# Turning half of the attention's probability units with VectorE blocks and a DRAM round trip

## The chip, the cores and the metric

The kernel runs on one core of one Trainium2 chip. The metric is the device time of one execution in microseconds (us). Three runs of the kernel before gave 720.13, 720.44 and 720.46 us, a median of 720.44 us. The engines are named as the profile names them: PE is TensorE (PEld its weight loads), DVE is VectorE, ACT is ScalarE, POOL is GpSimd, and SP issues the DMAs; SPq is the DMA queue of SP.

## What is computed

Attention over a few global keys and a local window, then a mixture of four experts, then a gated layer with a norm. The change touches the attention alone, but the experts' matmuls are woven into the same stretch.

```python
def _attn_ref(q, k, v, n_global, n_local):          # B=2, H=8, S=768, D=64; 8 global keys, window of 96
    scores = scale * np.matmul(q, k.transpose(0, 1, 3, 2))
    keep = is_global | is_local
    scores = np.where(keep, scores + bias, -1e9)
    a = np.exp(scores - np.max(scores, axis=-1, keepdims=True))
    a = a / (np.sum(a, axis=-1, keepdims=True) + 1e-09)
    return np.matmul(a, v)

def _moe_ref(x, domain_probs, w1, w2):              # N=1536, D=512, E=4, F=1024
    for e in range(E):
        out += p[:, e:e + 1] * (np.maximum(x @ w1[e], 0.0) @ w2[e])
```

## The kernel before, in words

The 1536 tokens are 12 slots of 128. A unit is one slot and one pair of heads, so there are 48 units, four for each slot: unit u belongs to slot u // 4 (from unit 8 on). For a unit, PE multiplies queries by 256 keys into the PSUM tile `sps` (`scores`, L1219); DVE adds the bias and takes the row extreme (L1270, one instruction for each head); ACT takes the exponential and the row sum (L1277); DVE sums and inverts (L1256, L1257) and scales the probabilities `p` (L1261, 128x512); PE turns the four 128x128 chunks through PSUM (`stage_b`, L1301) and ACT copies them to SBUF (L1303); PE multiplies them by the values into `x` (`stage_c`, L1323; each fp32 product is two instructions); after the fourth unit of a slot ACT and DVE split `x` into a high and a low part, `xh` (L1334) and `xl` (L1335).

From unit 14 (`PAIRS`) on the loop takes two units in one step: step t (t = 14, 16, ..., 50) issues the scores and the softmax of units t and t+1, scales and turns units t-2 and t-1, and multiplies units t-4 and t-3 by their values. Between these, `pull(share)` draws matmuls of the experts from a generator, worth `share` ns at full speed, and does so twice in a step. The order of each engine's instructions is the order of the program; nothing is reordered. So a step divisible by 4 (16, 20, ...) begins a slot, and a step that leaves 2 (18, 22, ...) ends one: there `stage_c` completes the slot before.

SP carries the loads in program order. At the start of a step divisible by 4, `next_operands` loads keys (`load_keys`, L90, two DMAs, by the table LOAD_AFTER) and the queries (L1188) of a later slot. The keys lie in a ring of four places; keys 6 to 9 also need their first 32 columns, which POOL copies from the place of key 6 (L93). Key 6 is loaded in step 20. At the end of a step that leaves 2, `load_v` (L1193) loads a later slot's values into one of two buffers. From step 36 on POOL forms sums for the experts (`x_forms`, L799), a few at the end of each step.

Near the end of the kernel, `blocks` (L1036 to L1043) turns a 128x1024 tile in the same way as the change does: one DVE transpose in 32x32 blocks (L1038), one DMA to `t_dram` (L1040), four DMAs back (L1042).

Of the kernel before, what the change touches and what calls it, by code (L numbers as in the profile page):

```python
# [8 lines left out]
F32 = mybir.dt.float32  # L9
# [36 lines left out]
SHARE = {11: 1000}  # L46
HALF = 512
PAIRS = 14


@with_exitstack
def kernel(ctx, tc, ep, qk, vp, nn, pr, wall, w64, gl, out):
# [1094 lines left out]
    def fast_arm():  # L1147
        st = stream("f")
        with ExitStack() as es:
# [4 lines left out]
            b0 = tmp2.rearrange("p a (h c) -> p (a h) c", c=128)  # L1154
            qp = enter(tc.tile_pool(name="qp", bufs=3))
            vpl = enter(tc.tile_pool(name="vpl", bufs=2))
            pp = enter(tc.tile_pool(name="pp", bufs=4))
            ptp = enter(tc.tile_pool(name="ptp", bufs=4))
            ss = enter(tc.tile_pool(name="ss", bufs=4))
            hA = enter(tc.tile_pool(name="hA", bufs=4))  # L1160
            psg = enter(tc.tile_pool(name="psg", bufs=3, space=PSUM))
# [63 lines left out]
            def soft(u, first):  # L1225

                s, pr_ = unit(u)
                nch, boff, _ = geom(s)
                nw = 128 * nch
                p = pp.tile([128, 2, 256], F32, tag="p", name="p")  # L1230
                mn = ss.tile([128, 2], F32, tag="mn", name="mn")
                st_p[u], st_rs[u] = p, sum_of(u)
                norm = stage_n(u - 1) if st_rs.get(u - 1) is not None else iter(())
                if not first:
                    next(norm, None)
                for a in range(2):
                    h = 2 * pr_ + a
                    bias = b0[:, h] if boff is None else btab[:, h, boff:boff + 256]
                    nc.vector.tensor_tensor_reduce(out=p[:, a, :nw], in0=sps[:, a, u % 2, :nw], in1=bias, scale=-0.125,
                                                   scalar=3.0e38, op0=ALU.add, op1=ALU.min,  # L1240
                                                   accum_out=mn[:, a:a + 1])
                    if not first:
                        while a and late:
                            late.pop()()
                        next(norm, None)
                for a in range(2):
                    nc.scalar.activation(p[:, a, :nw], p[:, a, :nw], AF.Exp, bias=mn[:, a:a + 1], scale=-1.0,
                                         accum_out=st_rs[u][:, a, 0:1])
                return norm

            def soft_pair(t):

                if PAIRS < t <= NU:
                    st_rs.pop(t - 2), st_rs.pop(t - 1)
                    su = ss.tile([128, 4], F32, tag="su2", name="su2")
                    nc.vector.tensor_reduce(out=su, in_=sums[:, (t // 2 - 1) % 3], op=ALU.add, axis=AX.X)  # L1256
                    nc.vector.reciprocal(out=su, in_=su)  # L1257
                    for u in (t - 2, t - 1):
                        p = st_p[u]
                        st_last[0] = p[:, 0, 0:1]  # L1260
                        nc.vector.tensor_tensor(out=p, in0=p, in1=su[:, 2 * (u % 2):2 * (u % 2) + 2].unsqueeze(2)  # L1261
                                                .to_broadcast([128, 2, 256]), op=ALU.mult)
                for u in (t, t + 1) if t < NU else ():
                    s, pr_ = unit(u)
                    boff = geom(s)[1]
                    st_p[u] = p = pp.tile([128, 2, 256], F32, tag="p", name="p")
                    st_rs[u] = sum_of(u)
                    mn = ss.tile([128, 2], F32, tag="mn", name="mn")
                    for a in range(2):
                        nc.vector.tensor_tensor_reduce(out=p[:, a], in0=sps[:, a, u % 2],  # L1270
                                                       in1=btab[:, 2 * pr_ + a, boff:boff + 256], scale=-0.125,
                                                       scalar=3.0e38, op0=ALU.add, op1=ALU.min,
                                                       accum_out=mn[:, a:a + 1])
                    while late:
                        late.pop()()
                    for a in range(2):
                        nc.scalar.activation(p[:, a], p[:, a], AF.Exp, bias=mn[:, a:a + 1], scale=-1.0,  # L1277
                                             accum_out=st_rs[u][:, a, 0:1])
# [15 lines left out]
            def stage_b(u):  # L1294
                s, pr_ = unit(u)
                nch = geom(s)[0]
                p = st_p.pop(u)
                pt = psT.tile([128, 4, 128], F32, tag="pt", name="pt")
                for a in range(2):
                    for c in range(nch):  # L1300
                        nc.tensor.transpose(pt[:, nch * a + c], p[:, a, 128 * c:128 * c + 128], ident)  # L1301
                t = ptp.tile([128, 4, 128], F32, tag="pts", name="pts")
                nc.scalar.copy(t[:, :2 * nch], pt[:, :2 * nch])  # L1303
                st_pt[u] = t

            def stage_c(u):
                s, pr_ = unit(u)
                nch, _, parts = geom(s)
                t = st_pt.pop(u)
                if u < N0:  # L1310
                    x, place = x0[:, 2 * (pr_ % 2):2 * (pr_ % 2) + 2], s
                else:
                    if pr_ == 0:
                        st_x[s] = psX.tile([128, 4, 128], F32, tag="x", name="x")
                    x, place = st_x[s], pr_
                for c in range(nch):
                    for a in range(2):
                        h = 2 * pr_ + a
                        if s < NAT:
                            v = v0[:, s, 64 * h:64 * h + 64]  # L1320
                        else:
                            v = vts[s][:, parts[c], 64 * h:64 * h + 64]
                        nc.tensor.matmul(x[64 * a:64 * a + 64, place], lhsT=v, rhs=t[:, nch * a + c],  # L1323
                                         start=(c == 0), stop=(c == nch - 1))
                if u < N0 and s == NAT - 1:
                    xc = slice(pr_, pr_ + 1), slice(0, 128 * NAT)
                elif u >= N0 and pr_ == 3:
                    xc = slice(0, 4), slice(128 * s, 128 * s + 128)
                else:
                    return  # L1330
                h_, l_ = xh[:, xc[0], xc[1]], xl[:, xc[0], xc[1]]
                if u < N0:
                    x = x.rearrange("p s c -> p (s c)").unsqueeze(1)
                nc.scalar.copy(h_, x)  # L1334
                late.append(lambda: nc.vector.tensor_tensor(out=l_, in0=x, in1=h_.bitcast(F32), op=ALU.subtract))  # L1335
# [198 lines left out]
                    st.split_piece("act" if t < N0 + 12 and t % 2 else "dve", "pool")  # L1534
                    st.load_piece()
            for t in range(PAIRS, NU + 3, 2):
                share = 2 * (EARLY if t < N0 + 27 else 750)
                if t < NU:
                    for u in (t, t + 1):
                        scores(u)  # L1540
                    for u in (t, t + 1):
                        next_operands(*divmod(u, 4))
                soft_pair(t)
                while late:
                    late.pop()()
                while st.rests:
                    st.rests.pop(0)()
                if t <= NU:
                    st.behind = False
                    pull(share)  # L1550
                for _ in range(2):
                    next(rest_p, None)
                if t <= NU:
                    for u in (t - 2, t - 1):
                        stage_b(u)
                if t < NU:
                    tokens[0] = 128 * done
                    st.behind = t < NU - 2
                    if t > PAIRS:
                        pull(share)  # L1560
                for u in (t - 4, t - 3):
                    if u in st_pt:
                        stage_c(u)
                if t % 4 == 2:
                    done = (t - 2) // 4
                    load_v(done + 1)
                if t == 4 * 8 + 4:
                    st.forms = st.x_forms(lambda: [tmp2[:, k] for k in range(2)])
                if st.forms and t < NU:
                    nc.gpsimd.tensor_copy(out=flg[:, 0:1], in_=st_last[0])  # L1570
                    for f in st.forms.pop(0):
                        f()
                if t < NU:
                    for u in (t, t + 1):
                        st.split_piece("act" if u < N0 + 12 and u % 2 else "dve", "pool")
                        st.load_piece()
# [180 lines left out]
```

## Time and profile before

| what | value |
|---|---|
| median of the runs | 720.44 us |
| profiled execution, its time | 720.14 us |
| profiled execution, its span from first to last instruction | 718.3 us |
| granted TensorE clock over the span | 1.000 |
| busy share of PE, DVE, ACT, POOL | 99%, 71%, 43%, 45% |
| steps 16 to 50 of the attention | from about 37 to 127 us of the span |

The span is 1.9 us shorter than the execution's time; that remainder lies around the instructions. The chain that ended last is followed back from the last instruction. The timeline gives start and duration of each instruction, merged where the same ones follow each other; a busy PE is modelled, so the start of the next instruction tells more than the end of one. In a row, the bracket names how long the engine was idle before the instruction, and what ended that.

### The profile page before, as it was taken

The page shows a single profiled execution, that of the slowest core. Times are in us where ns is not written, and L with a number is a line of the kernel's source. Part 1 is how long each engine was busy: PE and PEld are TensorE (multiplying, and loading weights), DVE is VectorE, ACT ScalarE, POOL GpSimd, SP SyncE. Part 2 cuts the span into 40 slices and gives each one's busy share as a digit, 9 for nine tenths or more (in the row PEclk, how much of TensorE's full clock was granted, in tenths as well). Part 3 has the DMA queues.
Part 4 walks back from the last instruction along what each step waited for, and adds up shares of the span by engine and source line. Part 5 has one row for each costly group of instructions (what it writes and reads, how often), then busy time and mean ns, then how long its engine had stood idle before and what let it go on. Part 6 is the DMA issues. An engine that isn't in the chain of part 4 may idle for free.

```text
span 718.3 us, 11137 instructions
## 1 busy us (share of the span) xinstructions
PE 709.4 (99%) x3863; PEld 591.7 (82%) x3863; DVE 506.5 (71%) x1100; ACT 307.0 (43%) x688; POOL 323.2 (45%) x389
## 2 busy tenths in 40 slices
PE   7999999999999999999999999999999999999997
PEld 5788877888888889888888988888898888888886
DVE  6788857638785685676668578857965667778870
ACT  5877765422523333232343324325334324454452
POOL 6700143574793165228307423630735089555600
PEclk9999999999999999999999999999999999999999
DMA  8734311320352324234133323323232780334341
GB/s 250 169 119 133 119 45 45 103 73 18 116 170 65 108 76 125 73 102 114 51 118 104 101 74 117 118 74 104 93 98 74 267 347 1 122 114 132 108 128 49
DMA packets 55601, 79.32 MB, mean 110 GB/s; under 512 B 5744, under 2 KB 33648, under 8 KB 55536
## 3 DMA queue, kind: packets, MB, share of 16 engines
q1 hardware_dynamic: 54976, 78.10, 34.4%
q8 instruction: 32, 0.52, 0.3%
q10 hardware_dynamic: 560, 0.43, 0.2%
q14 instruction: 33, 0.27, 0.1%
HBM read 59.60 MB, written 18.90 MB: 109 GB/s over the span
## 4 chain that ended last, share of the span: by engine, by line
PE 97%; DVE 1%; ACT 1%; issue 0%; DVEq 0%
PE fg L582 37%; PE fg L759 19%; PE fo L1087 9%; PE fh L988 8%; PE fg L674 7%; PE fg L551 6%; PE x L1323 3%; PE sps L1219 3%; PE pt L1301 3%; PE g L1343 1%; PE wp L133 1%; DVE fg L687 1%; ACT fhh L643 1%; PE fh L1068 0%; PE sps L1212 0%
## 5 line engine op out<-in xcount | busy, mean ns | idle before, releaser
L582 PE MATMUL fg<-fhh,wV 128*128 128x512 f32 (+1 forms) x800 | 243.4, 384 | 0.4
L582 PEld LDWEIGHTS fg<-fhh,wV 128*128 128x128 f32 x800 | 148.3, 188 | 33.5 <-issue 3.3
L582 PE MATMUL fg<-fhl,wV 128*128 128x512 f32 (+1 forms) x400 | 149.1, 381 | 0.0
L582 PEld LDWEIGHTS fg<-fhl,wV 128*128 128x128 f32 x400 | 74.9, 188 | 15.2 <-DVE su L1257 0.3
L643 ACT ACTIVATE fhh<-fg 128x512 fp32r<-128x512 f32 x80 | 47.5, 598 | 66.6 <-DVE fg L769 40.3
L308 POOL TENSOR_TENSOR wR<-kr,wR 128x512 fp32r<-128x512 f32 (+1 forms) x28 | 29.0, 1060 | 97.0 <-ACT wR L300 97.0
L644 DVE SCALAR_TENSOR_TENSOR fhl<-fg,fhh 128x512 fp32r<-128x512 f32 x80 | 54.0, 686 | 6.9 <-ACT fhh L643 5.4
L601 POOL TENSOR_TENSOR scr<-scr,kr 128x512 f32<-128x512 f32 x24 | 31.0, 1291 | 61.4 <-DVE kr L600 61.4
L759 PE MATMUL fg<-xt,fwS 128*128 128x512 f32 x252 | 58.3, 389 | 0.0
L759 PEld LDWEIGHTS fg<-xt,fwS 128*128 128x128 f32 x252 | 47.3, 188 | 9.8
L759 PE MATMUL fg<-xh,wR 128*128 128x512 f32 x168 | 54.0, 389 | 0.0
L769 DVE TENSOR_TENSOR fg<-kr,fg 128x512 f32<-128x512 f32 x42 | 29.0, 693 | 33.0 <-PE fg L759 22.6
L596 DVE TENSOR_TENSOR fg<-fg,pb 128x512 f32<-128x512 f32 x59 | 40.9, 692 | 14.4 <-PE fg L582 13.4
L1277 ACT ACTIVATE p<-p,mn 128x256 f32<-128x256 f32 x68 | 33.9, 499 | 22.9 <-DVE mn L1270 22.8
L597 DVE TENSOR_TENSOR scr<-fg,scr 128x512 f32<-128x512 f32 x59 | 40.8, 692 | 2.0
L551 PE MATMUL fg<-xh,wR 128*128 128x512 f32 (+1 forms) x128 | 39.4, 373 | 0.0
L759 PEld LDWEIGHTS fg<-xh,wR 128*128 128x128 f32 x168 | 31.6, 188 | 6.5
L308 POOL TENSOR_TENSOR fwS<-kr,fwS 128x512 fp32r<-128x512 f32 x28 | 35.7, 1299 | 1.6 <-ACT fwS L300 1.6
L1087 PE MATMUL fo<-xt,fhh 128*128 128x512 f32 (+1 forms) x156 | 35.4, 375 | 0.0
L764 ACT COPY kr<-fg 128x512 f32<-128x512 f32 x42 | 24.2, 590 | 25.6 <-PE fg L759 25.6
L759 PE MATMUL fg<-xl,wR 128*128 128x512 f32 x84 | 32.7, 389 | 0.0
L1087 PEld LDWEIGHTS fo<-xt,fhh 128*128 128x128 f32 x156 | 27.6, 188 | 5.1
(283 smaller groups left out, 1492.3 us busy)
## 6 DMA issues: line engine op xcount, KB each, us to landing
w_dram<-fr SPq DMA_DIRECT2D x44, 256.0 KB, 2.5
kr<-in_wall_dram SPq DMA_DIRECT2D x42, 256.0 KB, 2.9
fr<-in_w_dram SPq DMA_DIRECT2D x32, 256.0 KB, 2.8
pb<-p_dram SPq DMA_DIRECT2D x22, 256.0 KB, 3.3
v<-in_vp_dram SPq DMA_DIRECT2D x10, 512.0 KB, 3.4
kr<-t_dram SPq DMA_DIRECT2D x32, 128.0 KB, 2.9
frawt<-in_wall_dram SPq DMA_DIRECT2D x14, 256.0 KB, 2.8
xt<-w_dram SPq DMA_DIRECT2D x6, 512.0 KB, 9.9
```

What stands on the lines that cost most here:

```text
L308: e.tensor_tensor(out=w[:, 1], in0=t, in1=w[:, 0].bitcast(F32), op=ALU.subtract)
L551: nc.tensor.matmul(ps[:, :n], lhsT=w[:, a, k], rhs=b[:, k, cols], start=(k == 0 and i == 0), stop=(k == 3 and i == 2))
L582: nc.tensor.matmul(ps[:, :n], lhsT=w[:, a, k], rhs=b[k], start=(i == 0), stop=(i == 11))
L596: nc.vector.tensor_tensor(out=ps[:, :n], in0=ps[:, :n], in1=pg, op=ALU.mult)
L597: nc.vector.tensor_tensor(out=a, in0=ps[:, :n], in1=a, op=ALU.add)
L643: nc.scalar.activation(th, src, AF.Relu)
L644: residuals.append(lambda: nc.vector.scalar_tensor_tensor(out=tl, in0=src, scalar=0.0, in1=th.bitcast(F32), op0=ALU.max, op1=ALU.subtract))
L674: nc.tensor.matmul(ps[:, q_ * q:q_ * q + q_], lhsT=w[:, a, j], rhs=x[b][j], start=(opens and q == j == m == 0), stop=(j == 1 and m == 2), ...
L759: nc.tensor.matmul(ps, lhsT=w[:, a, j], rhs=x[b][j], start=(i in (1, 2, 5) and j == 0 and m == 0), stop=(j == 1 and m == 2), skip_group_ch ...
L988: nc.tensor.matmul(ps[i], lhsT=left[i][x][j], rhs=right[i][j][:, y], start=(i in (1, 5, 2) and j == m == 0), stop=(j == 1 and m == 2), ski ...
L1087: nc.tensor.matmul(ps, lhsT=a[:, fc % 4], rhs=wo[fc][:, i % 2, c0:c0 + n], start=(fc == i == 0), stop=(fc == 7 and i == 2))
L1277: nc.scalar.activation(p[:, a], p[:, a], AF.Exp, bias=mn[:, a:a + 1], scale=-1.0, accum_out=st_rs[u][:, a, 0:1])
```

## The change

For units u with u % 4 < 2 and 16 <= u <= 45 (16 units, the first two of a slot) the chunks are no longer turned by PE and copied by ACT. POOL scales `p`, DVE transposes it in 32x32 blocks into one tile `blocks`, one DMA per two units writes that to DRAM, and four DMAs of the next step bring it back turned (`turn`, `turned_back`). `stage_c` of these units comes one step later, behind that of the other two units of the slot; so a step that leaves 2 now multiplies four units by their values and a step divisible by 4 none. Unit 3 of each slot is scaled by POOL too while t < 36. The load of values moves from the end of a step that leaves 2 to the start of the next, behind the four DMAs. The share of each `pull` becomes 325 higher in a step divisible by 4 and 325 lower in the others. The temporaries of `x_forms` move to other tiles, since `blocks` is `tmp2`. The tiles of `p` and of the turned chunks become parts of one tile each, with four places as before.

```diff
+FORMS = 36
+SHIFT = 325
...
+            ps_all = pp.tile([128, 4, 2, 256], F32, name="p")
+            pts_all = pp.tile([128, 4, 4, 128], F32, name="pts")
+            blocks = tmp2.rearrange("p a c -> p (a c)")
...
-                        nc.vector.tensor_tensor(out=p, in0=p, in1=su[:, 2 * (u % 2):2 * (u % 2) + 2].unsqueeze(2)
-                                                .to_broadcast([128, 2, 256]), op=ALU.mult)
+                        e = nc.gpsimd if turned(u) or (u % 4 == 3 and t < FORMS) else nc.vector
+                        e.tensor_tensor(out=p, in0=p, in1=su[:, 2 * (u % 2):2 * (u % 2) + 2].unsqueeze(2)
+                                        .to_broadcast([128, 2, 256]), op=ALU.mult)
...
+            def turned(u):
+
+                return u % 4 < 2 and PAIRS < u < NU
+
+            def turn(u0):
+                for u in (u0, u0 + 1):
+                    p, k = st_p.pop(u), 4 * (u % 2)
+                    nc.vector.transpose(out=blocks.rearrange("p (jj c q) -> p c jj q", jj=4, c=8)[:, k:k + 4],
+                                        in_=p.rearrange("p a (c jj f) -> p (a c) jj f", c=2, jj=4))
+                nc.sync.dma_start(out=t_dram[u0 // 4 % 2], in_=blocks)
+
+            def turned_back(u0):
+                t = pts_all[:, 0:2].rearrange("p u c q -> p (u c q)")
+                for jj in range(4):
+                    nc.sync.dma_start(out=t[32 * jj:32 * jj + 32].rearrange("r (i c) -> r i c", i=4),
+                                      in_=t_dram[u0 // 4 % 2].rearrange("(i r) (j c) -> j r i c", r=32, j=4)[jj])
+                t = t.rearrange("p (i c q) -> p c i q", i=4, c=8)
+                for u in (u0, u0 + 1):
+                    st_pt[u] = [t[:, 4 * (u % 2) + c] for c in range(4)]
...
-                share = 2 * (EARLY if t < N0 + 27 else 750)
+                share = 2 * (EARLY if t < N0 + 27 else 750) + (SHIFT if t % 4 == 0 else -SHIFT)
...
+                if turned(t - 4):
+                    turned_back(t - 4)
+                    load_v((t - 4) // 4 + 1)
                 soft_pair(t)
...
+                if turned(t - 2):
+                    turn(t - 2)
...
-                if t <= NU:
+                if t <= NU and not turned(t - 2):
                     for u in (t - 2, t - 1):
                         stage_b(u)
...
-                for u in (t - 4, t - 3):
-                    if u in st_pt:
-                        stage_c(u)
+                if not turned(t - 4):
+                    for u in (t - 4, t - 3) + ((t - 6, t - 5) if turned(t - 6) else ()):
+                        if u in st_pt:
+                            stage_c(u)
                 if t % 4 == 2:
                     done = (t - 2) // 4
+                if t == PAIRS:
                     load_v(done + 1)
```

## Rows read from the trace of the kernel before

**Rows 1.** The page: shares of the chain that ended last, by engine.
```profile
PE 97%; DVE 1%; ACT 1%; issue 0%; DVEq 0%
```
**Rows 2.** Stretches of two steps: length, busy PE, PEld, DVE, ACT, POOL, clock, DMA.
```profile
42.20:51.01 8.81, 8.81 (x88) 7.48 (x84) 7.29 (x27) 6.65 (x22) 0.00 (x0) 1.00 0.38 115
...
69.58:78.77 9.19, 9.19 (x91) 7.89 (x89) 7.54 (x28) 6.41 (x22) 0.00 (x0) 1.00 0.48 136
...
87.91:100.82 12.91, 12.91 (x94) 9.93 (x93) 8.63 (x27) 7.83 (x24) 6.55 (x7) 1.00 0.26 82
```
**Rows 3.** Timeline, PE in step 18: start, duration, engine, line.
```profile
41.85 1.14 PE L1219 MATMUL sps<-kr,q 64*128 64x256 f32 x8
...
42.92 0.39 PE L582 MATMUL fg<-fhh,wV 128*128 128x256 f32 x1
...
43.73 1.03 PE L1301 MATMUL pt<-ident,p 128*128 128x128 f32 x8
...
44.52 0.36 PE L582 MATMUL fg<-fhh,wV 128*128 128x256 f32 x1
44.72 0.29 PE L582 MATMUL fg<-fhl,wV 128*128 128x256 f32 x1
...
45.41 1.09 PE L1323 MATMUL x<-pts,v 128*64 128x128 f32 x16
...
46.44 1.14 PE L1219 MATMUL sps<-kr,q 64*128 64x256 f32 x8
```
**Rows 4.** Timeline, the softmax loop of step 18 on DVE.
```profile
42.20 0.16 DVE L1256 TENSOR_REDUCE su<-sums 128x4 f32<-128x8 f32 x1 [0.54 <-ACT p L1277]
...
42.62 1.29 DVE L1261 TENSOR_TENSOR p<-p,su 128x512 f32<-128x512 f32 x2
...
46.46 0.16 DVE L1256 TENSOR_REDUCE su<-sums 128x4 f32<-128x8 f32 x1 [0.84 <-ACT p L1277]
```
**Rows 5.** Timeline, PE and DVE in steps 46 to 50.
```profile
115.94 1.13 PE L1219 MATMUL sps<-kr,q 64*128 64x256 f32 x8
...
117.12 0.42 DVE L1270 CUSTOM_DVE_ANT_0 p<-sps,btab 128x256 f32<-128x256 f32 x1 [0.60 <-PE sps L1219]
...
120.87 1.09 PE L1323 MATMUL x<-pts,v 128*64 128x128 f32 x16
...
121.90 0.50 PE L582 MATMUL fg<-fhh,wV 128*128 128x512 f32 x1
...
125.07 1.97 PE L1323 MATMUL x<-pts,v 128*64 128x128 f32 x32
...
126.97 0.50 PE L582 MATMUL fg<-fhh,wV 128*128 128x512 f32 x1
```
**Rows 6.** Groups of DVE (late stage) and POOL (attention): count, busy us, mean ns.
```profile
L1038 DVE STREAM_TRANSPOSE pb<-scr 128x1024 f32<-128x1024 f32 x4 | 5.0, 1246 | 0.1
...
L799 POOL TENSOR_TENSOR scr<-xh,xl 128x512 f32<-128x512 f32 x3 | 3.8, 1283 | 0.0
```
**Rows 7.** Timeline: a POOL sum and the DVE scaling that begins under it.
```profile
87.80 1.29 POOL L799 TENSOR_TENSOR tmp<-tmp,xh 128x512 f32<-128x512 f32 x1
...
88.32 1.32 DVE L1261 TENSOR_TENSOR p<-p,su 128x512 f32<-128x512 f32 x1
```
**Rows 8.** Timeline, SP's queue and POOL in step 20.
```profile
46.95 1.19 SPq L90 DMA_DIRECT2D kr<-in_qk_dram  x2
48.19 1.26 SPq L1188 DMA_DIRECT2D q<-in_qk_dram  x2
...
51.35 0.29 POOL L93 COPY kr<-kr 128x128 f32<-128x128 f32 x1 [18.42 <-DMA kr<-in_qk_dram]
```
**Rows 9.** The late stage's DRAM round trip: SP's timeline, and landing after issue.
```profile
637.43 0.33 SPq L1040 DMA_DIRECT2D t_dram<-scr  x1
640.10 1.75 SPq L1042 DMA_DIRECT2D kr<-t_dram  x4
...
DMA to landing us min/median/max: 2.5/2.9/3.6
```

More of the change, by code (lines that the diff above doesn't have):

```diff
@@ L1156, in fast_arm @@
             vpl = enter(tc.tile_pool(name="vpl", bufs=2))
-            pp = enter(tc.tile_pool(name="pp", bufs=4))
-            ptp = enter(tc.tile_pool(name="ptp", bufs=4))
+            pp = enter(tc.tile_pool(name="pp", bufs=1))
+            ps_all = pp.tile([128, 4, 2, 256], F32, name="p")
+            pts_all = pp.tile([128, 4, 4, 128], F32, name="pts")
+            blocks = tmp2.rearrange("p a c -> p (a c)")
             ss = enter(tc.tile_pool(name="ss", bufs=4))
@@ L1229, in soft @@
                 nw = 128 * nch
-                p = pp.tile([128, 2, 256], F32, tag="p", name="p")
+                p = ps_all[:, u % 4]
                 mn = ss.tile([128, 2], F32, tag="mn", name="mn")
@@ L1265, in soft_pair @@
                     boff = geom(s)[1]
-                    st_p[u] = p = pp.tile([128, 2, 256], F32, tag="p", name="p")
+                    st_p[u] = p = ps_all[:, u % 4]
                     st_rs[u] = sum_of(u)
@@ L1301, in stage_b @@
                         nc.tensor.transpose(pt[:, nch * a + c], p[:, a, 128 * c:128 * c + 128], ident)
-                t = ptp.tile([128, 4, 128], F32, tag="pts", name="pts")
+                t = pts_all[:, u % 4]
                 nc.scalar.copy(t[:, :2 * nch], pt[:, :2 * nch])
-                st_pt[u] = t
+                st_pt[u] = [t[:, c] for c in range(2 * nch)]
+            def turned(u):
[14 more added lines that the diff above has]
+                    st_pt[u] = [t[:, 4 * (u % 2) + c] for c in range(4)]
             def stage_c(u):
@@ L1312, in stage_c @@
                 else:
-                    if pr_ == 0:
+                    if s not in st_x:
                         st_x[s] = psX.tile([128, 4, 128], F32, tag="x", name="x")
@@ L1322, in stage_c @@
                             v = vts[s][:, parts[c], 64 * h:64 * h + 64]
-                        nc.tensor.matmul(x[64 * a:64 * a + 64, place], lhsT=v, rhs=t[:, nch * a + c],
+                        to, r = x[64 * a:64 * a + 64, place], t[nch * a + c]
+                        if turned(u):
+                            to = to.rearrange("p (i q) -> p i q", i=4)
+                        nc.tensor.matmul(to, lhsT=v, rhs=r,
                                          start=(c == 0), stop=(c == nch - 1))
@@ L1326, in stage_c @@
                     xc = slice(pr_, pr_ + 1), slice(0, 128 * NAT)
-                elif u >= N0 and pr_ == 3:
+                elif u >= N0 and pr_ == (1 if turned(u) else 3) and not turned(u - 2):
                     xc = slice(0, 4), slice(128 * s, 128 * s + 128)
@@ L1560, in fast_arm @@
                         pull(share)
-                for u in (t - 4, t - 3):
-                    if u in st_pt:
-                        stage_c(u)
+                if not turned(t - 4):
+                    for u in (t - 4, t - 3) + ((t - 6, t - 5) if turned(t - 6) else ()):
+                        if u in st_pt:
+                            stage_c(u)
                 if t % 4 == 2:
                     done = (t - 2) // 4
+                if t == PAIRS:
                     load_v(done + 1)
-                if t == 4 * 8 + 4:
-                    st.forms = st.x_forms(lambda: [tmp2[:, k] for k in range(2)])
+                if t == FORMS:
+                    st.forms = st.x_forms(lambda: [st.rawp.tile([128, 512], F32, tag="raw", name="fraw")
+                                                   for k in range(2)])
                 if st.forms and t < NU:
```

## The prediction

> **What bounds the kernel now.** I read the page first, then the stretches of the attention, then the timeline. PE is busy for 99% of the span, by the table above, and holds 97% of the chain that ended last [rows 1]; in the attention it is busy in every microsecond, at the full granted clock, while DVE has 7.3 of 8.8 us and POOL nothing [rows 2]. The timeline of step 18 shows what a step is: scores at 41.85, the experts' matmuls, the eight transposes from 43.73 to 44.52, experts again, 16 value matmuls at 45.41, and the next scores at 46.44 [rows 3]. So each PE instruction removed here should shorten the kernel, if nothing else takes its place. The second bound is close: in the same step DVE's loop (sum, inverse, scaling, biases, then ACT's exponentials, then the next sum) lasts 46.46 - 42.20 = 4.26 us, of which DVE idles only 0.84 behind ACT [rows 4]; the PE step lasts 4.59. There is room of some 10%, not more.
>
> **What goes.** 16 units lose four PE transposes each, 64 in eight groups of eight. A group takes 44.52 - 43.73 = 0.79 us [rows 3], so 6.3 us. Two value groups now follow each other: 16 alone take 121.90 - 120.87 = 1.03, 32 together 126.97 - 125.07 = 1.90 [rows 5], which saves 0.16 for each of eight slots, 1.3 us. At a seam PE loses a little: the first expert matmul behind the transposes takes 44.72 - 44.52 = 0.20 [rows 3], where 256 columns at 2.4 GHz are 0.11. One or two seams a slot go; I add 0.05 for each slot. Sum: 8.0 us, between 6.3 and 8.4. The value matmuls now read their columns in pieces of 32, which no row shows. The nearest are the scores, whose keys lie in two pieces: 42.92 - 41.85 = 1.07 for 8 x 256 columns, 0.52 ns each, against 1.03 for 16 x 128 of the values, 0.50 [rows 3, 5]. So between nothing and 4% of eight groups, 0.3 us; I take nothing, and a gain there has no reason. The expert work is the same in sum: the shares' +325 and -325 cancel over steps 14 to 48. ACT loses 16 copies, which nothing waited for.
>
> "VectorE: DVE Perf Modes", section "Rules for kernel authors", of the Trainium skill speaks against this change: it gives a full 128x128 transpose to TensorE and leaves VectorE the 32x32 blocks alone. Its figure for a TensorE transpose, 390 ns, would by that page make 64 of them an estimated 25 us; in the trace they are pipelined and cost 0.1 us each [rows 3], and that decides: the rule prices one transpose, not the engine that is full.
>
> **What comes on DVE and POOL.** DVE loses two scalings of 0.65 (1.29 for two [rows 4]) in each step that leaves 2 and gains two 128x512 block transposes, half of 1.246 [rows 6], 0.63 each: even. POOL takes two scalings of about 1.29 there [rows 6] and, before step 36, one in each step divisible by 4. That last one starts together with DVE's scaling of unit 2. The trace shows what happens then: POOL's sum held 87.80 to 89.09, and DVE's scaling, begun at 88.32, took 1.32 instead of 0.65, ending 0.55 after POOL [rows 7]; two operations that each read two SBUF tiles run one after the other. Whichever is second, unit 3 is scaled 2.3 us after the sum instead of 1.7, and PE reaches it about then. I put 0.4 us on step 16 and 0.1 on each of four later steps.
>
> **The chain of the turned values.** Let S be the start of the scores in a step that leaves 2. The biases wait for both units' scores, 117.12 - 115.94 = 1.2 [rows 5], and four take 1.45: S+2.6. The two POOL scalings end at S+2.9 to 3.8, as the sum comes 0.3 before S or 0.6 behind. The second transpose then ends, and the write is issued, at S+3.9 to 4.5. The late stage shows the same transfers: reads 2.67 us behind the write, four issues in 1.75, landing 2.9 after the last issue began [rows 9]: 6.9 us, so S+10.8 to 11.4. (The key and query loads, 1.19 + 1.26 us of issuing [rows 8], fit between write and reads.) PE wants the values in the next step that leaves 2, behind the scores (1.07), two small pulls (0.42 each) and the other two units (0.85): 2.76 after its start. Two steps last 9.1 us now [8.81 and 9.19, rows 2] and 8.1 with 1.0 less, so S+10.9. Late by 0 to 0.6; I take 0.3 for each of four slots before step 38. From step 38 on two steps last over 10 us [12.91, rows 2], and nothing is late. With the scalings above, 2.0 us; bounds 0.5 and 4.
>
> **Step 20.** In that step POOL's queue holds the copy of key 6 ahead of the scaling of unit 19. Now that copy waits for its load until 51.35 and delays no one [rows 8]. After the change SP issues the load behind the new DRAM write, which waits for the transposes of step 18. Step 18 starts near 42.1; its sum is ready near 41.65, POOL ends both scalings at 44.75, DVE transposes until 46.1, the write is issued, and the two key loads go at 46.5, against 46.95 now. The copy then ends at 50.95 + 0.3, the scaling of unit 19 at 52.6. PE, with 1.07 of scores, 1.2 of experts and unit 18's transposes, is there at 47.8. It waits 4.8 us with everything behind it in its queue (unit 19's transposes, the experts, the scores of step 22). The load's issue fixes the end, so being early elsewhere does not help. Bounds 3.5 and 5.6; I take 4.9. Keys 7, 8 and 9 copy from key 6's place, long loaded, and wait for scores of the step before: no cost.
>
> **The end.** In step 50 no experts are drawn. Step 46 starts its scores at S; the write is issued at S+4.05, the reads land at S+10.9. PE has 1.07, two pulls of 1.27, four value groups 1.9, a pull of 1.97, transposes 0.8, then units 46 and 47, which now follow their own copies at once: ready at S+9.3 to 9.6. It waits 1.6 in all (0.5 to 3) where there is no wait now, since the values of units 44 and 45 fill it.
>
> **How the numbers follow.** 720.14 (the profiled execution) - 8.0 + 2.0 + 4.9 + 1.6 = 720.6; the median of the runs stands 0.3 above that execution, so 720.9. A difference under 0.2%, 1.44 us, can't be told from none. This forecast's own range is 718.3 to 723.4, and it has half of the chance: 0.06 below 719.0, 0.32 within, 0.12 above 721.88.
>
> **Rival 1: step 20 doesn't wait.** If key 6 lands early, or PE has enough else to do, 4.9 falls away: 716.0 (715 to 718). For it speaks that the load waits only for SP's queue; against it, that the write stands ahead in that queue and a key load took over 3 us to reach POOL [rows 8]. Chance 0.26.
>
> **Rival 2: the DRAM trip sets the pace.** Each 0.1 us by which the write comes later than S+4.5, or the trip lasts longer than 6.9, is paid in four early slots and at the end. At a trip of 7.9 us (landings reach 3.6 [rows 9], and keys, queries and values load at the same time) that is 5 x 0.8 = 4: 725 (722.5 to 727). It decides from about 7.3 us on. Against it: slots in step with the trip let DVE and POOL catch up. Chance 0.14.
>
> **Rival 3: the clock falls in step 20.** PE was granted 1.00 in all stretches and never stood so long in the attention [rows 2]; no row tells what a wait of 4.9 us does. At half of the clock each microsecond of work costs another: 2.7 if it lasts for the rest of step 20 (transposes 0.4, experts 1.2, scores 1.07), 4.6 if for the whole step behind it: 723.6 to 725.5. "TensorE: Matmul & The Clock Gate", Part 1, of the Trainium skill says that an idle array falls to 1.2 GHz. No run here shows it. Chance 0.1, nearly all slower.
>
> Faster is then 0.06 + 0.26 = 0.32; within 0.33; slower 0.12 + 0.14 + 0.09 = 0.35. For 8 in 10 the range takes in the middle of rival 1 and most of rival 2: 716.0 to 724.8.
>
> **What would show it.** Right: POOL's scaling behind the key copy in step 20, with PE idle 4 to 5.5 us before the transposes at unit 19; the first value matmul on returned chunks idle 0 to 0.6 us on a DMA in steps 26 to 34 and over 1 us in step 50; two steps of 8.1 to 8.5 us; 112 transposes left on PE; DVE transposes of 0.63; the granted clock at 1.00. Wrong: no idle time in step 20 (rival 1), waits on the DMA of over 0.8 us in each slot (rival 2), a lower granted clock (rival 3), or value matmuls slower than 53 ns each, which would reach past the range's upper side only together with rival 2.

## The result and the profile after

The changed kernel takes 727.73 us (median of 4 runs, 727.60 to 729.42) against 720.45 for the kernel before: a ratio of 1.0106, interval 1.0088 to 1.0123. It is slower, by 1.1%, and beyond the upper side of the range. The profiled execution took 727.78 us with a span of 726.0, so the span is 7.7 longer than before. Times here and below are medians of the fast executions; one of e3, 1014.86 us at a granted clock of 0.655, is left out.

The page of the kernel after: the granted clock in 40 slices of the span, and the shares of the chain that ended last.

```profile
PEclk9988999999999999999999999999999999999999
...
PE 92%; DMA 3%; DVE 2%; ACT 1%; issue 1%; SPq 0%; POOL 0%; DVEq 0%; POOLq 0%
```

Before, PE held 97% of that chain [rows 1]; now it holds 92%, and the DMA 3% that it did not have. Two slices of the attention are below full clock. What was added and removed is there as written. Groups of the kernel after, by line: count, busy time and mean ns.

```profile
L1266 POOL TENSOR_TENSOR p<-p,su 128x512 f32<-128x512 f32 x21 | 23.2, 1120 | 34.8 <-DVE su L1261 24.0 <-ACT pts L1308 5.6 <-PE sps L1223 5.2
...
L1306 PE MATMUL pt<-ident,p 128*128 128x128 f32 x112 | 17.0, 281 | 6.9 <-POOL p L1266 5.1 <-DVE p L1296 1.0 <-DVE p L1266 0.6
...
L1318 DVE STREAM_TRANSPOSE tmp<-p 128x512 f32<-128x512 f32 x16 | 10.5, 690 | 0.0
```

112 transposes are left on PE and 16 block transposes run on DVE. Where PE stood is in its view of waits (total, times, longest us):

```profile
PE pt L1306 <- POOL p L1266: 5.1, 1, 5.1
PE x L1351 <- DMA pts<-t_dram: 4.6, 3, 2.1
...
PE pt L1306 <- DVE p L1266: 0.6, 1, 0.6
PE x L1351 <- ACT pts L1308: 0.3, 1, 0.3
```

The timeline of PE in the kernel after shows the places, in steps 20, 26, 34 and 50:

```profile
47.61 0.60 PE L1306 MATMUL pt<-ident,p 128*128 128x128 f32 x4
53.35 1.12 PE L1306 MATMUL pt<-ident,p 128*128 128x128 f32 x4 [5.14 <-POOL p L1266]
...
70.46 1.47 PE L1351 MATMUL x<-pts,v 128*64 128x128 f32 x16 [2.11 <-DMA pts<-t_dram]
...
90.97 1.09 PE L1351 MATMUL x<-pts,v 128*64 128x128 f32 x16 [1.88 <-DMA pts<-t_dram]
...
133.30 1.09 PE L1351 MATMUL x<-pts,v 128*64 128x128 f32 x16 [0.64 <-DMA pts<-t_dram]
```

Since ends are modelled, I count from start to start, less the normal pitch: 5.3 us in step 20, 2.3 in step 26, 2.0 in step 34, 0.8 in step 44 (on DVE's scaling), 0.5 and 0.8 in step 50; 11.7 in all. Before, no gap in that stretch exceeds the pitch by 0.4.

The rest is the clock. Stretches of the kernel after; columns as in [rows 2], with the granted clock third from the end:

```profile
48.00:53.40 5.40, 0.26 (x3) 0.06 (x1) 1.58 (x6) 2.35 (x9) 1.29 (x2) 0.74 0.80 211
53.40:57.60 4.20, 4.20 (x20) 3.95 (x22) 0.67 (x3) 0.59 (x1) 0.30 (x1) 0.53 0.52 149
57.60:61.00 3.40, 3.40 (x46) 2.75 (x42) 2.65 (x11) 2.08 (x8) 1.98 (x3) 1.00 0.00 0
...
70.40:74.20 3.80, 3.74 (x25) 2.62 (x26) 0.27 (x2) 0.59 (x1) 0.98 (x1) 0.58 0.70 220
88.80:92.00 3.20, 1.32 (x23) 0.94 (x19) 2.97 (x7) 0.98 (x5) 0.03 (x1) 1.00 0.99 318
```

In step 20 the clock fell while PE stood (0.74 in the first row). Behind that wait PE works for 4.2 us at 0.53, which is the lower level of 1.2 GHz nearly throughout; the lost work is 0.47 x 4.2 = 2.0 us. Behind the wait in step 26 it is 0.42 x 3.8 = 1.6. Waits and clock make 15.3 us; the span grew by 7.7, so the removed work saved about 7.6. That figure is a remainder: it holds every small error of the others.

### The profile page after: what moved, and what is told of

Same layout as the page of the kernel before. It is cut to its first block, busy times and chain, and to the rows that moved or that the text cites. A ratio compares the mean times of both kernels' runs of the same rounds, so it can differ in the third digit from the quotient of the medians.

```text
span 726.0 us, 11061 instructions
## 1 busy us (share of the span) xinstructions
PE 706.6 (97%) x3799; PEld 587.9 (81%) x3799; DVE 502.9 (69%) x1095; ACT 299.8 (41%) x672; POOL 346.1 (48%) x410
## 4 chain that ended last, share of the span: by engine, by line
PE 92%; DMA 3%; DVE 2%; ACT 1%; issue 1%; SPq 0%; POOL 0%; DVEq 0%; POOLq 0%
PE fg L584 36%; PE fg L761 18%; PE fo L1089 9%; PE fh L990 8%; PE fg L676 7%; PE fg L553 5%; PE sps L1223 3%; PE x L1351 2%; PE pt L1306 2%; DMA pts<-t_dram 2%; PE g L1371 1%; PE wp L135 1%; DMA kr<-in_qk_dram 1%; DVE fg L689 1%; ACT fhh L645 1%
## 5 line engine op out<-in xcount | busy, mean ns | idle before, releaser
L1266 POOL TENSOR_TENSOR p<-p,su 128x512 f32<-128x512 f32 x21 | 23.2, 1120 | 34.8 <-DVE su L1261 24.0
L1275 DVE CUSTOM_DVE_ANT_0 p<-sps,btab 128x256 f32<-128x256 f32 x68 | 25.3, 420 | 14.8 <-PE sps L1223 14.8
```

## The experiments

My theory after this reading: step 20's wait costs itself and the clock behind it, and the DRAM trip is late where steps are short because the slot's loads share the DMA with it. The rivals: the clock falls for another reason (the DMA's traffic, say); the trip is late because of step 20's disturbance alone; the trip is too slow wherever it stands.

The rows of a run are those of its one profiled execution. In e1, e2, e5, e6, e7 and e10 that execution took 1.0 to 2.0 us longer than the median, so waits read from its rows and differences of medians agree only that closely.

### One moved scaling by itself: e3_before_unit19 and e8_before_unit19

The kernel before, with one instruction elsewhere:

```diff
-                        nc.vector.tensor_tensor(out=p, in0=p, in1=su[...]
+                        e = nc.gpsimd if u == 19 else nc.vector
+                        e.tensor_tensor(out=p, in0=p, in1=su[...]
```

> The kernel before, with one thing of the change alone: unit 19 is scaled by POOL. It stands behind the copy of key 6 there too, which ended at 51.64 us. Theory: POOL scales from 51.7 to 52.7, PE reaches unit 19's transposes at 48.7 and waits 4 us, nothing gives that back, and behind the wait the granted clock falls to one half for about 4 us, 2 us more: 724.0 to 726.8. Rival one: the wait costs what it lasts and the clock's fall needs the DMA load of the changed kernel: 724 to 724.8. Rival two: the order on POOL costs nothing: 720.4.

Measured: 727.68 us (727.15 to 729.30), ratio 1.0107, interval 1.0090 to 1.0124; more than the theory's 724.0 to 726.8. One instruction of about 1 us on an engine that was idle costs as much as the whole change. For its rows the kernel ran once more:

> The kernel before with unit 19 alone scaled by POOL, once more for its trace: PE waits 4 to 4.8 us in step 20 ahead of unit 19's transposes, the granted clock is at one half for 3 to 5 us behind that and at 1.00 elsewhere; 727 to 728.

Measured: 726.8 us in one execution, a little under the range, span 725.0, 6.7 above the span before. PE's timeline in step 20 of this kernel:

```profile
48.43 0.60 PE L1302 MATMUL pt<-ident,p 128*128 128x128 f32 x4
53.82 1.12 PE L1302 MATMUL pt<-ident,p 128*128 128x128 f32 x4 [4.79 <-POOL p L1262]
```

and its stretches around it:

```profile
50.00:53.00 3.00, 0.00 (x0) 0.00 (x0) 1.80 (x5) 1.14 (x5) 0.53 (x2) 1.00 0.50 133
53.00:56.00 3.00, 2.18 (x10) 2.10 (x10) 0.00 (x0) 0.59 (x1) 0.77 (x1) 0.58 0.01 3
56.00:60.00 4.00, 4.00 (x38) 3.31 (x37) 1.31 (x7) 0.78 (x3) 0.29 (x1) 0.89 0.00 0
```

A gap of 5.0 us beyond the pitch; then PE works for 2.18 us of the second row at 0.50, which costs 1.1, and the third row costs 0.11 x 4 = 0.4. That makes 6.5 of the 6.7. While the clock is down the DMA moves nothing (0.01 and 0.00), so its traffic is not the cause; the idle PE is what remains, and e4 tests that. No DRAM write stands in SP's queue here, yet the wait is as long: it is the POOL queue, not the write ahead of the load.

### The same wait, filled: e4_fill_wait

The kernel after, with 20 matmuls that nobody reads ahead of unit 19's transposes:

```diff
+                if u == 19:
+                    for _ in range(20):
+                        nc.tensor.matmul(pt.rearrange("p a c -> p (a c)"), lhsT=warm[:, 0:128], rhs=warm,
+                                         start=True, stop=True)
```

> The changed kernel with 20 idle matmuls of 512 columns (about 4.5 us, on zeros, their result overwritten) ahead of unit 19's transposes: PE works through the wait of step 20 and the wait stays. Theory: the clock fell because PE stood still; it stays at 1.00 from 53 to 58 us, and 2.0 us go: 725.4 to 726.2. Rival: the clock falls there for another reason: 727.7 as before, or more where the filling outlasts the wait.

Measured: 724.74 us (724.49 to 726.57), ratio 1.0067, interval 1.0050 to 1.0084; 3.0 less than the kernel after, and less than the 725.4 expected at best. PE's timeline of this kernel in step 20, and two stretches of it:

```profile
47.83 0.60 PE L1310 MATMUL pt<-ident,p 128*128 128x128 f32 x4
48.18 4.82 PE L1306 MATMUL pt<-xl 128*128 128x512 f32 x20
53.56 0.66 PE L1310 MATMUL pt<-ident,p 128*128 128x128 f32 x4 [0.56 <-POOL p L1266]
```
```profile
47.00:53.00 6.00, 6.00 (x33) 4.83 (x31) 2.79 (x11) 2.66 (x9) 0.78 (x2) 1.00 0.78 225
53.00:57.00 4.00, 3.44 (x28) 2.92 (x28) 0.89 (x4) 0.59 (x1) 1.31 (x2) 1.00 0.66 193
```

Unit 19's transposes are as late as before (53.56 against 53.35), but the clock stays at 1.00. So the clock falls with the idle time, as the theory has it. Its part of step 20's 7.3 us is not the whole 3.0, though: counted from step 20 on, the scores of step 24 come 1.8 us earlier than in the kernel after (13.84 instead of 15.64 behind those of step 20), which agrees with the 2.0 of the rows. The rest comes later: in step 26 PE waits 1.66 us and not 2.11, and the clock stays at 1.00 there; a new wait of 1.33 in step 30 takes part of it back.

### The wait in step 20 taken away: e1_copy_behind

The kernel after; POOL's copy of the key is issued behind the scaling of unit 19:

```diff
-            nc.gpsimd.tensor_copy(out=kr[:, :, p, 0:32], in_=kr[:, :, NI % RING, 128:160])
+            copies.append(lambda: nc.gpsimd.tensor_copy(out=kr[:, :, p, 0:32], in_=kr[:, :, NI % RING, 128:160]))
...
                 soft_pair(t)
+                while copies and t % 4 == 0:
+                    copies.pop(0)()
```

> The changed kernel with one thing moved: POOL's copy of the key columns is queued behind the scaling of unit 3 of a slot, no longer ahead of it. Theory: in step 20 PE waited 5.4 us because unit 19's scaling stood behind a copy that waited for the load of key 6, and the clock fell by half behind that wait for some 4 us, 2 us more. So the gap falls to under 1 us, the clock stays at 1.00 there, and 7.3 us go; but steps 18 to 22 are then 5 us nearer to each other, and the values of units 16 and 17 come back from DRAM some 13 us after the scores of step 18, which is up to 2.5 us late in step 22. Together 720.5 to 724. Rival: the wait of step 20 is that of unit 19's softmax or of DVE, and stays: 727 to 728.

Measured: 723.54 us (720.46 to 724.88), ratio 1.0030, interval 1.0012 to 1.0048. The wait in step 20 is gone, and 4.2 us with it, but not the 5.3 and the clock behind it. The waits of PE in this kernel:

```profile
PE x L1353 <- DMA pts<-t_dram: 7.1, 4, 3.7
```

They were 4.6 in the kernel after. The longest, in step 30, is again followed by the low clock (0.50 from 77 to 81 us). SP's timeline there:

```profile
65.47 0.34 SPq L1322 DMA_DIRECT2D t_dram<-tmp  x1
65.91 4.09 SPq L94 DMA_DIRECT2D kr<-in_qk_dram  x4
70.05 1.26 SPq L1194 DMA_DIRECT2D q<-in_qk_dram  x2
71.42 1.96 SPq L1327 DMA_DIRECT2D pts<-t_dram  x4
```

The reads go out 5.95 us behind the write, as four key loads and two query loads stand between; in the late stage it was 2.67 [rows 9]. Step 20's wait had given the DMA time; without it the trip is the bound. The rival that lays the late trip on step 20 alone falls. The five executions lie 4.4 us apart, with a granted clock over the span of 0.998 in the fastest and 0.993 to 0.994 in the others.

### Which transfers make the trip late: e2_loads_early, e5_spread, e9_no_loads, e11_act_queue

All four are the kernel e1 with the loads arranged otherwise. e2 loads keys, queries and values a step earlier, behind the scores of the step that ends a slot:

```diff
-                    for u in (t, t + 1):
-                        next_operands(*divmod(u, 4))
+                    if t % 4 == 2:
+                        next_operands((t + 2) // 4, 0)
+                        if t > PAIRS + 4:
+                            load_v((t - 2) // 4)
                 if turned(t - 4):
                     turned_back(t - 4)
-                    load_v((t - 4) // 4 + 1)
```

> As the one before, and the loads of keys, queries and values are issued one step earlier, behind the scores of the step that ends a slot, so that SP's queue and the DMA engines have nothing else between the DRAM write and the four reads. Theory: the turned values came over 2 us late in steps 26 and 34 because write, reads and the loads (1 MB for each slot) share the queue in the same 5 us; reads then land 2.9 us after issue, as in the late stage, 11 us after the scores and not 13.3, and the waits on the DMA fall to under 0.6 us each: 713 to 716.5. Rival: the trip is as long by itself (write landing, four reads of 1 KB pieces), and the waits stay at about 2 us each: 719 to 723.

Measured: 727.42 us (726.59 to 728.93), ratio 1.0092, interval 1.0075 to 1.0109: 3.9 worse than e1 and above both forecasts, and PE waits 11.2 us for returned chunks. SP's timeline of e2 tells why:

```profile
63.78 2.50 SPq L94 DMA_DIRECT2D kr<-in_qk_dram  x4
66.33 1.26 SPq L1194 DMA_DIRECT2D q<-in_qk_dram  x2
67.64 0.60 SPq L1199 DMA_DIRECT2D v<-in_vp_dram  x1
68.33 0.38 SPq L1322 DMA_DIRECT2D t_dram<-tmp  x1
74.55 1.75 SPq L1327 DMA_DIRECT2D pts<-t_dram  x4
```

The reads wait for the write, and now that wait is 6.2 us: seven loads with 1.25 MB, issued in the 4.5 us before, stand ahead of it. Nothing stands between write and reads any more, and it is worse. e5 puts the keys there and the queries and values behind the reads:

```diff
-                    for u in (t, t + 1):
-                        next_operands(*divmod(u, 4))
+                    if t % 4 == 2:
+                        for j in LOAD_AFTER.get((t + 2) // 4 - 1, ()):
+                            load_keys(j)
                 if turned(t - 4):
                     turned_back(t - 4)
+                if t < NU and t % 4 == 0:
+                    load_q(t // 4 + 2)
+                if turned(t - 4):
                     load_v((t - 4) // 4 + 1)
```

> The kernel with the key copy behind the scaling, and the loads parted: keys behind the scores of the step that ends a slot, the DRAM write and the four reads with nothing between or just ahead of them, queries and values behind the reads. Theory: a trip is long because other loads of the slot lie ahead of it in the same queue (ahead of the reads in the changed kernel, ahead of the write with all loads early, where the write took 6 us instead of 2.7); parted, the write lands in 2.7 to 3.0, the reads 2.9 behind the last issue, and waits on the DMA are under 0.8 us in each slot: 714.5 to 718. Rival: the early slots move 2 MB in 8 us, which is about what the DMA engines carried at their fullest stretch here (231 to 318 GB/s), so the waits stay whatever the order: 719 to 723, with a DMA share over 0.9 from 50 to 90 us.

Measured: 724.69 us (723.17 to 725.88), ratio 1.0050, interval 1.0033 to 1.0067; above both forecasts and no better than e1. The waits are 7.7 us, and the reads still go out 5.3 to 5.6 us behind the write in three of the short slots and 4.3 in a fourth, but 2.7 behind it in the first slot and the fifth after it, where little else is loaded. e9 leaves the loads of queries and values out:

```diff
-                if 3 <= s < NSLOT:
+                if 6 <= s < NSLOT:
+                    qs[s] = qs[s - 3]
+                    return
+                if 3 <= s < NSLOT:
...
-                if s < NSLOT:
+                if 5 <= s < NSLOT:
+                    vts[s] = vts[s - 2]
+                elif s < NSLOT:
```

> The kernel with the key copy behind the scaling, and without the loads of queries from slot 6 and of values from slot 5 on (those slots use the tiles of earlier ones, so the output is not the reference's); the keys are still loaded. It takes 768 KB for each slot off the queue and leaves the trip through DRAM as it is. Theory: the trip was late because the slot's other loads share its queue and the DMA engines; the write now lands 2.7 us after issue in every slot, the reads 2.9 after theirs, no wait on the DMA is over 0.6 us, the clock stays at 1.00: 714 to 717. Rival: the trip is too long by itself in steps of 4 us, or PE is held by the loop of DVE, ACT and POOL: waits of 1.5 us or more stay in the slots before step 38: 719 to 722.

Measured: 717.60 us (717.17 to 718.01), ratio 0.9956, interval 0.9942 to 0.9969. Its waits on returned chunks, and the landing of its writes:

```profile
PE x L1358 <- DMA pts<-t_dram: 2.6, 4, 0.9
```
```profile
DMA to landing us min/median/max: 2.6/3.0/3.1
```

Without the loads of queries and values every write lands in 2.6 to 3.1 us, the clock stays at 1.00, and 5.9 us of e1's time are gone: the trip isn't too slow as such, it is late in company. (The time lies 0.6 above the range; three early waits of 0.6 to 0.9 us remain, where none over 0.6 was expected.) Whether the order of SP's queue does it or the DMA engines that all queues share is asked by e11, which is e5 with one word changed:

```diff
-                nc.sync.dma_start(out=t_dram[u0 // 4 % 2], in_=blocks)
+                nc.scalar.dma_start(out=t_dram[u0 // 4 % 2], in_=blocks)
```

> The kernel of e5_spread, but the DRAM write of the turned units goes out on ACT's queue, no longer behind the loads in SP's; every transfer and every byte stays. The write becomes ready at about the end of the exponentials of the same step, so ACT is held up little. Theory 1 (the order in SP's queue makes the write late): the write lands 2.6 to 3.5 us behind its issue in slots 5 to 7 too, instead of 5.3 to 5.6; the waits on returned chunks shrink from 7.7 us to 1 to 3, and the time is 718 to 721. Theory 2 (the 16 DMA engines are shared and full, whatever queue a transfer is in): the write still takes over 4.5 us, or it lands early and the reads and loads behind it land later by as much; waits 6 to 8 us, 723.5 to 726.

Measured: 721.07 us (719.93 to 722.91), ratio 0.9996, interval 0.9981 to 1.0010: 3.6 below e5, with the same transfers. Two writes of its timeline with the reads that wait for them:

```profile
53.24 1.19 SPq L94 DMA_DIRECT2D kr<-in_qk_dram  x2
...
53.90 0.35 ACTq L1322 DMA_DIRECT2D t_dram<-tmp  x1
59.65 3.11 SPq L1327 DMA_DIRECT2D pts<-t_dram  x4
...
76.47 0.33 ACTq L1322 DMA_DIRECT2D t_dram<-tmp  x1
...
79.87 1.73 SPq L1327 DMA_DIRECT2D pts<-t_dram  x4
```

Behind the write the reads of the early slots now wait 5.75, 4.4, 3.4 and 5.2 us, where e5 had 5.3, 5.6, 5.6 and 4.3: two are shorter by 1.2 and 2.2, two longer by 0.4 and 0.8. So on a queue of its own a write can still take as long as behind the loads, and the order of SP's queue is not all of it; that the DMA engines, which all queues share, hold it is then what is left, not shown by itself. The larger gain lies ahead of the write. In steps 22, 26, 30 and 34 it went out 4.6, 7.2, 5.3 and 5.7 us after the step's first scores in e5, and 3.9, 4.6, 3.9 and 3.9 in e11, as it no longer stands behind SP's issues of reads, queries, values and keys. Both theories hold in part: the waits of PE are 5.5 us, between the two forecasts, and the time lies at the edge of the first.

"DMA: Bandwidth & Descriptors", section "Issuing engines are not separate DMA queues", of the Trainium skill says that DMAs of all engines interleave on the same 16 DMA engines, and that a second issuer saves only the time to initiate them, usually small. e11 agrees, as its writes still took up to 5.7 us to land; but the saving, 0.7 to 2.6 us in a slot, was not small here, since the write stood in line behind 9 to 11 other issues of SP.

### Where the change pays: e6_late_only, e7_late_filled, e10_late_from_28, e12_late28_act

e6 turns only units 32 to 45, with the shares shifted from step 34 on, no unit 3 on POOL, and the values of the other slots loaded where the kernel before loads them:

```diff
-                return u % 4 < 2 and PAIRS < u < NU
+                return u % 4 < 2 and LATE <= u < NU
...
-                        e = nc.gpsimd if turned(u) or (u % 4 == 3 and t < FORMS) else nc.vector
+                        e = nc.gpsimd if turned(u) else nc.vector
```

> The changed kernel with the way through DRAM only for units 32 to 45 (four slots of eight), the shifted shares from step 34 on, no scaling of unit 3 by POOL; units 16 to 29 as before. Theory: a slot that is turned saves 1.0 us of PE, and from step 34 on two steps are longer than the trip, so no wait on the DMA over 0.5 us there; lost are the end (1.4 us) and the wait of 0.8 us in step 44: 720.4 - 4.0 + 2.2 = 718.6, between 717.5 and 719.3, clock 1.00. Rival: the saving is smaller than counted, or the trip's own cost (DVE's transposes, POOL's scalings ahead of its sums) comes back later: 720 or more.

Measured: 718.91 us (718.03 to 719.97), ratio 0.9977, interval 0.9967 to 0.9988. That is within the forecast. The only wait on the DMA left is 1.8 us in step 50. e7 gives PE expert work there, a second pull in step 48:

```diff
-                if t < NU:
+                if t <= NU:
                     tokens[0] = 128 * done
                     st.behind = t < NU - 2
                     if t > PAIRS:
                         pull(share)
```

> The same with a second draw of the experts' matmuls in step 48, between the transposes of units 46 and 47 and the values of units 44 to 47. Theory: the 1.4 us at the end are a wait for ACT's copies and for the trip, which 2 us of experts cover: 1.3 us less than the one before, 716.5 to 717.7. Rival: the wait at the end moves to the experts' evictions or to the next block: no difference.

Measured: 718.39 us (717.34 to 721.95), ratio 0.9973, interval 0.9961 to 0.9986. It is faster than the kernel before by 2.1 us (0.3%) and than the kernel after by 9.3. Of the 1.3 us that the second pull was to give, 0.5 came, which the spread of the two runs does not tell from none: the wait for chunks in step 50 fell from 1.8 to 0.6, and a wait of 0.5 before the experts is new, as the rival had it in part. PE's waits on returned chunks and on DVE in it:

```profile
PE x L1352 <- DMA pts<-t_dram: 0.6, 1, 0.6
PE pt L1307 <- DVE p L1267: 0.6, 1, 0.6
PE fg L554 <- DVE xl L1364: 0.5, 1, 0.5
```

e10 is e7 with one slot more, `LATE = 28`, the last one of the short steps:

> The late version with the second draw in step 48, and units 28 and 29 turned as well (five slots). Theory: slot 7 is still in the short steps, where the trip meets the loads of four keys, queries and values; it comes 1.5 to 3 us late in step 34 and takes back more than the 1.0 us of the transposes: 718.4 to 720.5, so no gain over the version from unit 32 on. Rival: the step that is half short leaves room enough: 717.3.

Measured: 720.63 us (718.83 to 722.65), ratio 0.9999, interval 0.9984 to 1.0014. In the profiled execution (722.58) that one slot waits 3.1 us for its chunks, more than it saves, and the clock falls behind the wait (0.50 from 85 to 88 us). e12 is e10 with the write on ACT's queue:

> The kernel of e10_late_from_28 with the DRAM write on ACT's queue. Theory 1: the wait of 3.1 us on the returned chunks of slot 7 in step 34 falls under 1 us, as its write no longer stands behind loads and its reads can start earlier; 717.3 to 718.5. Theory 2: the write stood behind little here (its own issue came before the keys), so its landing was not the delay; the reads still queue behind keys and queries on SP, and the wait stays at 2.5 to 3.5 us; 720 to 721.

Measured: 719.08 us (717.84 to 719.83), ratio 0.9972, interval 0.9960 to 0.9984; the wait on the chunks is 1.8 us, between the two forecasts, and the clock stays at 1.00 behind it. It is no better than e7.

## Why the prediction was wrong

**What goes (-8.0): right as far as is known.** About 7.6 as the remainder of the account; e6, forecast with 1.0 us for each slot, came out 0.3 from its forecast.

**Step 20 (+4.9): right, 5.3.** POOL's timeline in the kernel after:

```profile
52.00 0.29 POOL L95 COPY kr<-kr 128x128 f32<-128x128 f32 x1 [7.25 <-DMA kr<-in_qk_dram]
52.25 1.04 POOL L1266 TENSOR_TENSOR p<-p,su 128x512 f32<-128x512 f32 x1
```

The loads went out at 46.73, as forecast (46.5). They reached POOL 5.3 us later, not after the 4.4 of [rows 8] (e8, without a write ahead: 47.08 to 52.47, 5.4); against that the scaling took 1.04 and not 1.29.

**The end (+1.6): right, 1.3.** In e7 expert work took 1.2 us out of the wait for chunks there, of which 0.5 at most came back in the time.

**The clock (rival 3, chance 0.1): the step that failed first.** I had the wait of 4.9 us at a chance near one half and then treated the clock behind it as a separate accident, because no row showed one. Where a wait of 5 us is forecast, the fall of the clock belongs in the sum: it fell behind each of the seven waits of over 3 us in these runs. Its price was in the text, 2.7 to 4.6; measured were 2.0 behind step 20 and 1.6 behind step 26, 3.6 us in all for a term that the sum had at nothing. What the prediction cited from "TensorE: Matmul & The Clock Gate", Part 1, of the Trainium skill (an idle array falls to 1.2 GHz) agrees with these rows, 0.53 of 2.4 GHz over 4.2 us.

**The chain of the turned values (+2.0, of it 0.3 a slot): mis-sized, and in the wrong way.** The write went out at 61.07, S+4.1 for S = 56.95, as forecast. The rest by SP's timeline after:

```profile
61.07 0.34 SPq L1320 DMA_DIRECT2D t_dram<-tmp  x1
61.50 1.26 SPq L92 DMA_DIRECT2D kr<-in_qk_dram  x2
62.81 1.31 SPq L1192 DMA_DIRECT2D q<-in_qk_dram  x2
64.23 1.96 SPq L1325 DMA_DIRECT2D pts<-t_dram  x4
66.23 0.55 SPq L1197 DMA_DIRECT2D v<-in_vp_dram  x1
```

Reads 3.16 behind the write, not 2.67; four issues in 1.96, not 1.75; and the chunks used at 70.46, some 4.7 after the last issue began, not 2.9. The trip lasted 9.4 us instead of 6.9, and PE waited 2.3 in step 26 and 2.0 in step 34. The step that failed is the row it was priced by: [rows 9] stand in a stage where the queue carried little else. "Fit between write and reads" counted the issue time of the loads and not what they do to the landing of the write: without the queries and values no wait is over 0.9 us (e9). Rival 2 named keys, queries and values, but gave the trip one microsecond more; it was 2.5 here and 4.9 in step 30 of e1 (write at 65.47, use at 77.22), where the trip sets the pace. Two of the four early slots, those of steps 22 and 30, were not late in the kernel after, where the waits ahead of them had lengthened their steps; in e1, without the wait of step 20, PE waits 2.2 and 3.7 there. The scalings' 0.8, by contrast, showed as no wait of PE in steps 16, 24, 28 and 32.

**The sum.** It gave +0.5 for the profiled execution, and its span grew by 7.7. Of the 7.2 us between, the clock is 3.6, the chain 2.3 (4.3 in steps 26 and 34 for 2.0), step 44 is 0.8, and what goes, step 20 and the end make the remaining 0.5. I added the terms as if each stood alone. e1 shows they don't: with 5.3 us of wait and its clock taken out, the kernel gained 4.2, as waits on the DMA grew from 4.6 to 7.1 and the clock fell behind one of them. Rival 1's 716.0 would not have come true either: without the wait in step 20 the trip is what is late next, and 723.54 is what that gave.

**Not foreseen at all:** 0.8 us in step 44, where the first pull drew nothing and PE came to its transposes before DVE had scaled.

What stays open is, first, when the clock falls behind a short wait. In the kernel after it fell behind the wait in step 26 (2.11 us in the row) and not behind that in step 34 (1.88). The length alone does not decide it: in e2 it stayed at 1.00 behind a longer wait, as this row of PE and the stretch that begins with it show.

```profile
79.08 1.09 PE L1353 MATMUL x<-pts,v 128*64 128x128 f32 x16 [2.51 <-DMA pts<-t_dram]
79.08:83.00 3.92, 3.92 (x40) 3.37 (x41) 1.72 (x8) 1.68 (x5) 0.52 (x1) 1.00 0.84 216
```

Second, it is open how the loads and the write share the DMA engines: e11's early slots lie between 3.4 and 5.75 us without a rule that I could see.

## What to carry to other kernels

Moving work to an idle engine costs what stands in that engine's queue, so read the queue's order, above all instructions that wait for a load; one scaling behind one copy cost about 7 us here (e3, e8). Price a round trip through DRAM by rows in which the same queue carries the same other loads, or put it only where there is slack of the size of those loads. When a forecast contains a wait of PE, ask what the clock behind it is worth and what becomes late next once the wait is removed; the terms of such a sum are not independent.

## What the runs showed of the hardware

- Behind a wait of 5 us PE ran at half of its clock for about 4 us (0.53 in 53.40 to 57.60), and with the DMA idle too (e8). Matmuls that do nothing in that wait kept the clock at 1.00; the kernel took 3.0 us less, 1.8 of it by step 24 (e4). Behind PE's waits of 2.1 to 2.5 us in the attention the clock fell in three places (2.11 in the kernel after, 2.25 and 2.45 in e5) and not in two (2.18 in e1, 2.51 in e2).
- A 512 KB write lands in 2.6 to 3.1 us with little else in the queue, and lets its reads go only after 4.3 to 6.5 where 1 MB of loads or more was issued shortly before it (e2, e5, e9).
- POOL's scaling, one operand repeated along the row, took 1.04 us against 1.28 for its sum of two full tiles [rows 6] and 0.69 for the same scaling on DVE. Beside a scaling of DVE it took up to 1.46, as in [rows 7] a scaling of DVE took 1.32 under a sum of POOL.
